# Chunked attention, a gated MLP and a routed expert layer in one program: the first block's vector work in a fixed order

## Chip, cores and metric

The program runs on one core of a Trainium2 chip. The metric is device time in microseconds (us): the median of three runs of the whole program.

## The reference, cut to what matters

```python
# attention inside chunks of 64 tokens: q, k, v are [8, 8, 576, 64]
attn = softmax(q_c @ k_c.T / sqrt(64)) @ v_c          # 4608 tokens x 512
# a dense gated layer, w_in 512 x 2048, w_out 2048 x 512, both in float64
h = x @ w_in
g = h * (1.0 / (1.0 + np.exp(-1.702 * h)))
x = (g @ w_out).astype(np.float32)
# routed layer: tokens with x @ w_skip > 0 go through one of 8 experts
out[do_compute] = xc + gate_w * (relu(xc @ w1[e]) @ w2[e])
```

The change touches the dense layer's first block of tokens and the conversion of its float64 weights that runs beside it.

## The kernel before, in words

The 4608 tokens are cut into 9 blocks of 512. For every block `j` the dense layer runs 16 rounds `i`, one per 128 columns of `w_in`. A round is `emit_h` (12 matmuls of 512 columns into a PSUM bank, L296, then a tanh on ACT, L299, and a multiply on VectorE, L300, which give `sg`), `emit_g` (ACT rounds `sg` to a high part `gh`, L306; VectorE takes the low part `gl`, L307) and, one round later in the program's text, `emit_y` (8 matmuls with `gh`, L316 and L317, and 4 with `gl`, L320). Each product is made of three because values and weights are split into a high and a low part. There are two PSUM banks for `h`, so `h` of round i+2 can start only when L300 of round i has read its bank.

Attention of the next block goes along in some rounds (1, 4, 7, 10 and 13 of block 0). Around a round k of these stand: `a` in round k-1 (8 transposes on TensorE, L141, two copies on ACT, L143), `burst` in round k (the value products of the group before, L207, and the scores of this one, L158; then maxima and differences on VectorE, L166 and L168, the exponential on ACT, L173, and two copies on ACT, L212), and in round k+2 the normalisation `c0` on VectorE (L176 to L179) and `c1` (4 transposes on TensorE, L187, a copy on ACT, L189). All of these PSUM results share two banks, tag `at`.

In block 0 the 32 weight halves (`class Half`: even ones a slice of `w_in`, odd ones of `w_out`) are turned from float64 into two float32 parts, one step ("tick") each. A half needs a load of 512 KB on SP's queue (three buffers), `s0` (two ACT instructions: `r`, L255, and `lf`, L256), `s1` (VectorE shift, L262, and combine, L263, then an add on POOL, L264) and `s3` (ACT rounds to `whi`, L276; VectorE subtracts to `wlo`, L277). Tick m does `s1` of half m, `s0` of half m+1, `s3` of half m-1 and starts the load of half m+3. Before the change six ticks are named in the prologue, and two in each round of block 0 until the 33 are used up.

The program is built in a framework whose scheduler takes the instructions in the order named and may move them: each engine gets an order that the scheduler makes at build time from its own idea of when things are ready. On the chip every engine then runs its own list strictly from first to last.

Of the kernel before, what the change touches and what calls it, by code (L numbers as in the profile page):

```python
# [9 lines left out]
F32 = mybir.dt.float32  # L10
# [11 lines left out]
def kernel(  # L22
# [14 lines left out]
    PE, ACT, DVE, POOL, SP = nc.tensor, nc.scalar, nc.vector, nc.gpsimd, nc.sync  # L37
# [5 lines left out]
    P = 128  # L43
# [3 lines left out]
    NF = DFF // P  # L47
    BT = 512
    TPB = BT // P
# [11 lines left out]

    BURSTS = {0: (1, 4, 7, 10, 13)}
    BURSTN = (1, 5, 9, 13)
    NXT = NT // SL + NE + NSING + 2
    BIG = float(1 << 20)

# [4 lines left out]
    mp = ctx.enter_context(tc.tile_pool(name="main", bufs=1))  # L71
# [7 lines left out]
    def bank(shape, tag, name):  # L79
# [10 lines left out]
        fill=0.0, base=0, channel_multiplier=-1,  # L90
# [13 lines left out]
    emeta = cp.tile([1, 2, NE], U32, name="emeta")  # L104
    meta = cp.tile([1, 3, NXT], U32, name="meta")
    wgT = cp.tile([P, KD, NE + 1], F32, name="wgT")
# [123 lines left out]
    HW = KD * P  # L230

    class Half:
# [14 lines left out]
        def s0(self):  # L247
            bits = self.raw.bitcast(U32).rearrange("p (n two) -> p n two", two=2)
            self.hw = bits[:, :, 1]
            hwf = self.raw.bitcast(F32).rearrange("p (n two) -> p n two", two=2)[:, :, 1]  # L250
            self.r = mp.tile([P, HW], F32, tag="x2", name="r", bufs=4)
            self.lf = mp.tile([P, HW], F32, tag="junk", name="lf")


            ACT.activation(out=self.r, in_=hwf, func=AF.Abs, scale=2.0 ** -112)  # L255
            ACT.activation(out=self.lf.bitcast(U32), in_=bits[:, :, 0], func=AF.Copy, scale=2.0 ** -29)  # L256

        def s1(self):
# [3 lines left out]
            DVE.tensor_scalar(ru, ru, 3, None, op0=ALU.logical_shift_left)  # L262
            DVE.scalar_tensor_tensor(au, self.hw, 0x80000000, ru, op0=ALU.bitwise_and, op1=ALU.bitwise_or)  # L263
            POOL.tensor_tensor(au, au, self.lf.bitcast(U32), op=ALU.add)  # L264

        def s2(self):
            pass

        def s3(self):
            i, h = self.i, self.half  # L270
# [29 lines left out]
        DVE.scalar_tensor_tensor(sg, sg, 1.0, ps, op0=ALU.add, op1=ALU.mult)  # L300
        return sg

    def emit_g(sg):
        gh = mp.tile([P, BT], F32R, tag="gh", name="gh", bufs=2)
        gl = mp.tile([P, BT], F32R, tag="gl", name="gl", bufs=2)
        ACT.activation(out=gh, in_=sg, func=AF.Copy, scale=0.5)  # L306
        DVE.scalar_tensor_tensor(gl, sg, 0.5, gh.bitcast(F32), op0=ALU.mult, op1=ALU.subtract)  # L307
        return gh, gl

# [127 lines left out]
    def extras():  # L437
# [4 lines left out]
        def m2s(shape, nm, dt=F32):  # L442
            return m2.tile(shape, dt, name="x_" + nm)

        def wide(nm):
            t = m2.tile([P, DM], F32, tag="o", name=nm, bufs=2)
            return t[0:1, 0:NXT * NB2].rearrange("o (x b) -> o x b", b=NB2)

        xb = [1, NXT, NB2]
        rem, tu = m2s([1, NE], "rem"), m2s([1, NE], "tu", U32)  # L450
        bc, b0, b1 = m2s([1, 1, NB2], "bc"), m2s([1, 1, NB2], "b0"), m2s([1, 1, NB2], "b1")
        row0, dp = m2s([1, 1, NB2], "row0"), m2s([1, 1], "dp")
        ix, bj, cx = m2s([1, NXT, 1], "ix"), m2s([1, NXT, 1], "bj"), m2s([1, NXT, 1], "cx")

# [77 lines left out]
    def load_next():  # L532
        if cnt["load"] < len(wq):
            s, n, w = wq[cnt["load"]]
            cnt["load"] += 1
            single = s >= NFIRST + NPAIR and w == 0
            raw2.append((s, n, w, None if single else load_w2(expert(s), n, w)))
# [107 lines left out]
    fp = fstack.enter_context(tc.tile_pool(name="f64", bufs=1))  # L645

    def new_x1():
        return [mp.tile([P, 2, BT], F32, tag="x1", name="x1", bufs=2) for _ in range(2)]
# [24 lines left out]
    halves = [Half(m) for m in range(2 * NF)]  # L673
# [18 lines left out]
    tick_n = [0]  # L692

    def tick():
        m = tick_n[0]
        tick_n[0] += 1
        if m == 0:
            halves[0].s0()
        if m < 2 * NF:
            halves[m].s1()  # L700
        if 1 <= m <= 2 * NF:
            halves[m - 1].s2()
        if m + 1 < 2 * NF:
            halves[m + 1].s0()
        if 1 <= m <= 2 * NF:
            halves[m - 1].s3()
        if m + 3 < 2 * NF:
            halves[m + 3].load()

    for tau in range(TPB + 3):  # L710
        if 0 <= tau - 2 < TPB:
            A[tau - 2].c0()
        if tau < TPB:
            A[tau].a()
        if 0 <= tau - 1 < TPB:
            A[tau - 1].b()
        if 0 <= tau - 2 < TPB:
            A[tau - 2].c1()
        if 0 <= tau - 3 < TPB:
            A[tau - 3].d()  # L720
        if tau >= 1:
            tick()
    for g in range(2):
        SP.dma_start(out=tv[g], in_=z)
# [2 lines left out]
    fill, late = [], []  # L727
# [3 lines left out]
    for j in range(NB - 1):  # L731
        for i in BURSTS.get(j, BURSTN):
            round_of[j * NF + i] = len(round_of)
# [4 lines left out]
    for j in range(NB):  # L738
        lastb = j + 1 == NB
        if not lastb:  # L740
            x1 = new_x1()
        else:
            rs.close()
            rawp = rs.enter_context(tc.tile_pool(name="raw", bufs=2, side="right", reuse_waits="tile"))
            for _ in range(4):
                load_next()
        ys = [bank([P, DM], "y", "yps") for _ in range(TPB)]
        prev = None
        nf = len(fill)
        for i in range(NF):  # L750
            R = j * NF + i
            nc_ = round_of.get(R - 2)
            if nc_ is not None and nc_ < NST:
                St[nc_].c0()
            sg = emit_h(i, xh, xl)
            span = NF // 2 - 2 if lastb else NF - 5
            nfill = -(-len(fill) // (span - i)) if i < span else 0
            if nfill:
                fill.pop(0)()
                nfill -= 1  # L760
            if j == 0:
                tick()
                if i == 7:
                    gate_load()
                elif i == 11:
                    gate_rows()
            g = emit_g(sg)
            if prev is not None:
                emit_y(i - 1, prev, ys)
            na = round_of.get(R + 1)  # L770
            if na is not None and na < NST:
                St[na].a()
                if na + 1 < NST:
                    St[na + 1].load_qk()
            if nc_ is not None and nc_ < NST:
                St[nc_].c1()
            kb = round_of.get(R)
            if kb is not None:
                if kb:
                    St[kb - 1].x1 = x1  # L780
                burst(St[kb] if kb < NST else None, St[kb - 1] if kb else None)
                if kb < NST:
                    St[kb].load_v()
            if j == 0:
                tick()
            for _ in range(nfill):
                fill.pop(0)()
            if late and (i >= span or late[0][0] < j):
                late.pop(0)[1]()
            if lastb:  # L790
                if prev is not None:
                    conv_next2()
                if i == NF // 2:
                    gstack.close()
                    m2 = ctx.enter_context(tc.tile_pool(name="m2", bufs=1, reuse_waits="tile"))
                    for s in range(NEARLY):
                        slots[s].list(first_row(s))
                if i >= NF // 2 + 2 and i - NF // 2 - 2 < NEARLY:
                    slots[i - NF // 2 - 2].gather((NB - 1) * BT)
            prev = g  # L800
        if j == 0:
            while tick_n[0] <= 2 * NF:
                tick()
            fstack.close()
            gstack = ExitStack()
            gp = gstack.enter_context(tc.tile_pool(name="gates", bufs=1, reuse_waits="tile"))
            wg = gp.tile([P, NE, DM], F32, name="wg")
            ws = gp.tile([P, DM], F32, name="ws")
            SP.dma_start(out=ws, in_=w_skip.rearrange("(o d) -> o d", o=1).to_broadcast([P, DM]))
            SP.dma_start(  # L810
                out=wg, in_=wgd[0:NE].rearrange("(o e) d -> o e d", o=1).to_broadcast([P, NE, DM]))
        if not lastb:
            xhn = split_x1(x1)
            emit_y(NF - 1, prev, ys)
            xh, xl = xhn
        else:
            slots[0].trans()
            emit_y(NF - 1, prev, ys)
            conv_next2()
        xs = evac_y(j, ys)  # L820
        lg = new_lg()
        if not lastb:
            fill = [lambda t=t, e=e, lg=lg, xs=xs: dot(lg, xs, t, e) for t in range(TPB) for e in range(NE + 1)]
            rt = route(j, lg)
            if j == NB - 3:
                rt.insert(3, order)
            late += [(j + 1, f) for f in rt]


    jx = m2.tile([1, NXT, 1], F32, name="jx")  # L830
    jw = m2.tile([1, NXT, 1], F32, name="jw")
    jm = m2.tile([1, NXT, 1], F32, name="jm")
# [103 lines left out]
```

## Time and profile before

| what | value |
|---|---|
| time, three runs | 1224.11, 1224.36, 1226.07 us; median 1224.36 |
| profiled execution | 1227.84 us, of which the span is 1226.1 us |
| TensorE busy, share of the span | 1182.7 us, 96% |
| VectorE, ACT, POOL | 783.9, 490.2, 144.6 us |

The profiled execution is 3.48 us above the median of the runs. TensorE is near full from about 60 us to the end; the slices that are not full lie in the first 160 us, the prologue and block 0. Block 0's first `h` matmul stands at 48.73 us.

### The profile page before, as it was taken

Reading aid. Unit: us, or ns where it says so; the run is one execution under the profiler, and the core shown is the slowest. Engines: PE = TensorE matmul, PEld = TensorE weight load, DVE = VectorE, ACT = ScalarE, POOL = GpSimd, SP = SyncE. Lnnn points to the kernel's source line nnn. Section 1 sums busy time; section 2 is a strip of 40 time slices with the busy share of each in tenths; the row PEclk is TensorE's granted clock in tenths of the full one; section 3 lists DMA queues with packets and bytes.
Section 4 is the critical chain, followed back from the end, with each engine's and each line's share of the span. In section 5 each row is a group of like instructions: output and inputs, shape, how many; then the busy total and the mean of one; then the engine's idle time right before and its main releaser. Section 6 shows DMA issues by size and latency. Waiting matters only on the chain. (4 is left out here: it accounts for less than half of the span.)

```text
span 1226.1 us, 20893 instructions
## 1 busy us (share of the span) xinstructions
PE 1182.7 (96%) x7984; PEld 991.8 (81%) x7984; DVE 783.9 (64%) x1771; ACT 490.2 (40%) x825; POOL 144.6 (12%) x137
## 2 busy tenths in 40 slices
PE   6798999999999999999999999999999999999995
PEld 4576788888888888888888888888788989999885
DVE  5889578369349548647736935943985686665531
ACT  5867443343332333324334333332344454444320
POOL 2344000010010010000001001001021023231110
PEclk9999999999999999999999999999999999999998
DMA  9756331131122113113113113202344677666540
GB/s 211 208 175 178 112 102 27 44 104 26 27 68 78 28 31 107 32 31 95 35 36 104 26 28 92 55 10 69 130 139 131 215 170 265 215 228 227 195 144 8
DMA packets 181848, 129.00 MB, mean 105 GB/s; under 512 B 122336, under 2 KB 155360, under 8 KB 181617
## 3 DMA queue, kind: packets, MB, share of 16 engines
q1 hardware_dynamic: 177072, 117.09, 33.4%
q0 software_dynamic: 4672, 10.54, 2.5%
q8 instruction: 64, 1.05, 0.4%
q14 instruction: 40, 0.32, 0.1%
HBM read 103.59 MB, written 25.04 MB: 105 GB/s over the span
## 5 line engine op out<-in xcount | busy, mean ns | idle before, releaser
L316 PE MATMUL yps<-whi,gh 128*128 128x512 f32 x576 | 228.7, 397 | 6.4 <-ACT gh L306 6.4
L296 PE MATMUL hps<-xh,whi 128*128 128x512 f32 x576 | 231.6, 405 | 3.2 <-DVE sg L300 3.2
L296 PE MATMUL hps<-xl,whi 128*128 128x512 f32 x576 | 227.5, 395 | 0.0
L296 PE MATMUL hps<-xh,wlo 128*128 128x512 f32 x576 | 227.0, 394 | 0.0
L317 PE MATMUL yps<-wlo,gh 128*128 128x512 f32 x576 | 225.6, 392 | 0.0
L300 DVE SCALAR_TENSOR_TENSOR sg<-sg,hps 128x512 f32<-128x512 f32 x144 | 98.3, 684 | 172.1 <-ACT sg L299 171.1
L353 DVE CUSTOM_DVE_ANT_0 junk<-x,wg 128x512 f32<-128x512 f32 x256 | 175.8, 687 | 4.0
L543 DVE TENSOR_TENSOR elo<-rawe,ehi 128x1024 fp32r<-128x1024 f32 x88 | 107.6, 1224 | 84.6 <-ACT ehi L542 84.5
L320 PE MATMUL yps<-whi,gl 128*128 128x512 f32 x576 | 156.0, 393 | 0.0
L299 ACT ACTIVATE sg<-hps 128x512 f32<-128x512 f32 x144 | 85.8, 598 | 163.4 <-PE hps L296 163.2
L542 ACT CAST ehi<-rawe 128x1024 fp32r<-128x1024 f32 x88 | 92.3, 1049 | 139.6 <-PE h2p L608 69.4
L306 ACT ACTIVATE gh<-sg 128x512 fp32r<-128x512 f32 x144 | 91.0, 632 | 118.3 <-DVE sg L300 104.8
L316 PEld LDWEIGHTS yps<-whi,gh 128*128 128x128 f32 x576 | 108.3, 188 | 30.9 <-ACT gh L306 7.8
L296 PEld LDWEIGHTS hps<-xh,whi 128*128 128x128 f32 x576 | 108.5, 190 | 26.3 <-DVE sg L300 4.1
L296 PEld LDWEIGHTS hps<-xh,wlo 128*128 128x128 f32 x576 | 108.9, 189 | 22.6
L320 PEld LDWEIGHTS yps<-whi,gl 128*128 128x128 f32 x576 | 108.0, 189 | 22.6 <-DVE gl L307 0.3
L317 PEld LDWEIGHTS yps<-wlo,gh 128*128 128x128 f32 x576 | 108.5, 188 | 21.8
L296 PEld LDWEIGHTS hps<-xl,whi 128*128 128x128 f32 x576 | 109.2, 190 | 20.6
L307 DVE SCALAR_TENSOR_TENSOR gl<-sg,gh 128x512 fp32r<-128x512 f32 x144 | 99.0, 688 | 33.4 <-ACT gh L306 21.7
L406 POOL DMA_INDIRECT tab<-pr,pos x36 | 37.8, 1049 | 682.3 <-DVE st L166 335.0
L608 PE MATMUL h2p<-xT,ehi 128*128 128x256 f32 x640 | 117.2, 283 | 0.0
L608 PEld LDWEIGHTS h2p<-xT,ehi 128*128 128x128 f32 x640 | 101.9, 191 | 2.6
(172 smaller groups left out, 1520.5 us busy)
## 6 DMA issues: line engine op xcount, KB each, us to landing
rawe<-in_moe_w_dram SPq DMA_DIRECT2D x88, 512.0 KB, 4.0
v<-in_v_dram SPq DMA_DIRECT2D x144, 64.0 KB, 2.7
x2d<-x SPq DMA_DIRECT2D x36, 256.0 KB, 3.1
out_dram<-x SPq DMA_DIRECT2D x36, 256.0 KB, 3.8
q<-in_q_dram SPq DMA_DIRECT2D x32, 256.0 KB, 3.7
k<-in_k_dram SPq DMA_DIRECT2D x32, 256.0 KB, 3.7
raw<-in_moe_w_in_dram SPq DMA_DIRECT2D x16, 512.0 KB, 4.0
raw<-in_moe_w_out_dram SPq DMA_DIRECT2D x16, 512.0 KB, 3.3
```

The costliest lines, as they stand in the source:

```text
L296: PE.matmul(ps, a, b[:, kk], start=(n == 0), stop=(n == 3 * KD - 1))
L299: ACT.activation(out=sg, in_=ps, func=AF.Tanh, scale=0.851)
L300: DVE.scalar_tensor_tensor(sg, sg, 1.0, ps, op0=ALU.add, op1=ALU.mult)
L306: ACT.activation(out=gh, in_=sg, func=AF.Copy, scale=0.5)
L307: DVE.scalar_tensor_tensor(gl, sg, 0.5, gh.bitcast(F32), op0=ALU.mult, op1=ALU.subtract)
L316: PE.matmul(ys[t], gh[:, cs], wh, start=first, stop=False)
L317: PE.matmul(ys[t], gh[:, cs], wl, start=False, stop=False)
L320: PE.matmul(ys[t], gl[:, cs], wh, start=False, stop=last)
L353: DVE.tensor_tensor_reduce(junk, xs[t], wg[:, e, :] if e < NE else ws, 1.0, 0.0, ALU.mult, ALU.add, lg[:, t, e:e + 1])
L542: ACT.copy(out=hi, in_=raw)
L543: DVE.tensor_tensor(lo, raw, hi.bitcast(F32), op=ALU.subtract)
L608: PE.matmul(ps[:, f], a[:, c], self.xT[:, b, kk], start=(m == 0), stop=(m == 3 * KD - 1))
```

## The change

From the start of block 0 to its end ACT, VectorE and POOL keep their instructions in the order in which the program names them; TensorE and SP are still ordered by the scheduler. Eight ticks instead of six are named in the prologue; the other 25 are dealt evenly over rounds 0 to 14 of the 16 (two, two, one, two, two, one and so on). A round's first tick is named in two parts, `tick1` (`s1`) between `gh` and `gl` and `tick2` (`s3`, `s0`, load) after `gl`; a second tick follows the attention's copies and stands before `burst`. Odd halves get another buffer for `lf`.

```diff
+    NTICK0 = 8
...
-            self.lf = mp.tile([P, HW], F32, tag="junk", name="lf")
+            pool, tag = ((mp, "junk"), (fp, "lf"))[self.half]
+            self.lf = pool.tile([P, HW], F32, tag=tag, name="lf")
...
-    def emit_g(sg):
+    def emit_g(sg, between=None):
...
         ACT.activation(out=gh, in_=sg, func=AF.Copy, scale=0.5)
+        if between is not None:
+            between()
         DVE.scalar_tensor_tensor(gl, sg, 0.5, gh.bitcast(F32), op0=ALU.mult, op1=ALU.subtract)
...
+    def tick1():
         m = tick_n[0]
-        tick_n[0] += 1
         if m == 0:
             halves[0].s0()
         if m < 2 * NF:
             halves[m].s1()
+
+    def tick2():
+        m = tick_n[0]
+        tick_n[0] += 1
         if 1 <= m <= 2 * NF:
-            halves[m - 1].s2()
+            halves[m - 1].s3()
         if m + 1 < 2 * NF:
             halves[m + 1].s0()
-        if 1 <= m <= 2 * NF:
-            halves[m - 1].s3()
         if m + 3 < 2 * NF:
             halves[m + 3].load()
+
+    def ticks_by(i):
+
+        return min(2 * NF + 1, NTICK0 - (-(2 * NF + 1 - NTICK0) * (i + 1) // (NF - 1)))
...
         if tau >= 1:
+            tick()
+        if tau > TPB:
             tick()
...
+        inorder = ExitStack()
+        if j == 0:
+            assert tick_n[0] == NTICK0
+            inorder.enter_context(tc.manual_schedule(engines={ACT.engine, DVE.engine, POOL.engine}))
         for i in range(NF):
...
+            mid = None
             if j == 0:
-                tick()
...
+                if tick_n[0] < ticks_by(i):
+                    mid = tick1
+            g = emit_g(sg, mid)
+            if mid is not None:
+                tick2()
...
             if nc_ is not None and nc_ < NST:
                 St[nc_].c1()
+            while j == 0 and tick_n[0] < ticks_by(i):
+                tick()
...
-            if j == 0:
-                tick()
```

What this does to the engines' lists is seen at three places. In the changed kernel's lists some lines have other numbers: L258 and L259 are `r` and `lf`, L265 and L266 shift and combine, L309 is `gl`, L145, L191, L214 the attention's copies on ACT, L168 and L170 its maxima and differences, L318, L319 and L322 `y`, L189 the transposes of `c1`, L209 the value products.

ACT, the stretch that holds the copy of `c1`'s transposes. Before, around the second of these copies in block 0 (L189):

```order
L143 COPY kT<-kTp 128x512
L255 ACTIVATE r<-raw_1190 128x512
L306 ACTIVATE gh<-sg 128x512
L256 ACTIVATE lf<-raw_1162 128x512
L276 CAST whi<-a 128x512
L256 ACTIVATE lf<-raw_1190 128x512
L276 CAST whi<-a 128x512
L255 ACTIVATE r<-raw_1220 128x512
L299 ACTIVATE sg<-hps 128x512
L189 COPY qT<-pTp 128x512
L256 ACTIVATE lf<-raw_1220 128x512
L255 ACTIVATE r<-raw_1252 128x512
```

In the changed kernel, round 3 from its first tick on, and the head of round 4:

```order
L276 CAST whi<-a 128x512
L258 ACTIVATE r<-raw_662 128x512
L259 ACTIVATE lf<-raw_662 128x512
L145 COPY qT<-qTp 128x512
L145 COPY kT<-kTp 128x512
L191 COPY qT<-pTp 128x512
L276 CAST whi<-a 128x512
L258 ACTIVATE r<-raw_723 128x512
L259 ACTIVATE lf<-raw_723 128x512
L299 ACTIVATE sg<-hps 128x512
L306 ACTIVATE gh<-sg 128x512
```

Before, a tanh (L299) stood ahead of the copy; now the three attention copies stand together, and the tanh of round 4 stands behind them and behind a whole tick.

TensorE, the transposes of `c1` that this copy waits for. Before, the same group's transposes (L187) stand inside an `h`; after that `h` come a whole `y`, the rest of the next `h`, and only then the value products:

```order
L296 MATMUL hps<-xl,whi 128x512
L296 MATMUL hps<-xh,wlo 128x512
L187 MATMUL pTp<-ident,qT 128x128 x4
L296 MATMUL hps<-xh,whi 128x512
L296 MATMUL hps<-xl,whi 128x512
L296 MATMUL hps<-xh,wlo 128x512
L316 MATMUL yps<-whi,gh 128x512
```

In the changed kernel, between `h` of round 5 and `y` of round 3 ahead, and `h` of round 6 behind:

```order
L318 MATMUL yps<-whi,gh 128x512
L319 MATMUL yps<-wlo,gh 128x512
L322 MATMUL yps<-whi,gl 128x512 x4
L189 MATMUL pTp<-ident,qT 128x128 x4
L209 MATMUL sv_881<-qT,v 64x64
```

The transposes moved behind `h` of round 5 and `y` of round 3, and the value products now follow them at once.

VectorE, a round with two ticks and a burst. Before, around the second burst:

```order
L300 SCALAR_TENSOR_TENSOR sg<-sg,hps 128x512
L263 SCALAR_TENSOR_TENSOR a<-raw_940,r 128x512
L262 TENSOR_SCALAR r<-r 128x512
L277 TENSOR_TENSOR wlo<-a,whi 128x512
L307 SCALAR_TENSOR_TENSOR gl<-sg,gh 128x512
L263 SCALAR_TENSOR_TENSOR a<-raw_970,r 128x512
L262 TENSOR_SCALAR r<-r 128x512
L166 TENSOR_REDUCE st<-sv_853 128x4
L166 TENSOR_REDUCE st<-sv_854 128x4
L277 TENSOR_TENSOR wlo<-a,whi 128x512
L168 TENSOR_TENSOR qT<-sv_853,st 128x2x2x64
L168 TENSOR_TENSOR qT<-sv_854,st 128x2x2x64
```

In the changed kernel, round 4:

```order
L300 SCALAR_TENSOR_TENSOR sg<-sg,hps 128x512
L265 TENSOR_SCALAR r<-r 128x512
L266 SCALAR_TENSOR_TENSOR a<-raw_723,r 128x512
L309 SCALAR_TENSOR_TENSOR gl<-sg,gh 128x512
L277 TENSOR_TENSOR wlo<-a,whi 128x512
L265 TENSOR_SCALAR r<-r 128x512
L266 SCALAR_TENSOR_TENSOR a<-raw_773,r 128x512
L277 TENSOR_TENSOR wlo<-a,whi 128x512
L168 TENSOR_REDUCE st<-sv_881 128x4
L168 TENSOR_REDUCE st<-sv_882 128x4
L170 TENSOR_TENSOR qT<-sv_881,st 128x2x2x64
L170 TENSOR_TENSOR qT<-sv_882,st 128x2x2x64
```

Both ticks now stand ahead of the burst's four instructions, and each combine follows the shift of its own half.

## Rows read from the trace of the kernel before

**Rows 1.** Busy time by stretch: start:end, length, each engine's busy us, clock, DMA.

```profile
57.50:119.00 61.50, 54.54 (x345) 42.50 (x346) 56.80 (x87) 44.73 (x81) 30.94 (x20) 0.97 0.61 180
119.00:146.60 27.60, 26.87 (x189) 21.59 (x190) 17.39 (x29) 15.07 (x29) 3.08 (x3) 1.00 0.23 54
```

**Rows 2.** Timeline of TensorE: start, length, engine, line, operation, [idle before <- releaser].

```profile
78.88 0.50 PE L316 MATMUL yps<-whi,gh 128*128 128x512 f32 x1 [2.99 <-ACT gh L306]
...
79.92 0.63 PE L316 MATMUL yps<-whi,gh 128*128 128x512 f32 x1
```

**Rows 3.** Timeline of block 0's end and of its first L300.

```profile
57.54 1.27 DVE L300 SCALAR_TENSOR_TENSOR sg<-sg,hps 128x512 f32<-128x512 f32 x2
...
165.54 1.07 PE L320 MATMUL yps<-whi,gl 128*128 128x512 f32 x4
```

**Rows 4.** Timeline of the prologue's end, ACT, TensorE and VectorE.

```profile
41.67 0.67 ACT L255 ACTIVATE r<-raw 128x512 f32<-128x512 f32 x1 [1.04 <-DMA raw<-in_moe_w_out_dram]
...
43.73 1.12 PE L207 MATMUL pv<-bA,v 64*64 64x64 f32 x16 [2.58 <-ACT x L212]
...
47.25 1.15 ACT L285 CAST xh<-x 128x512 fp32r<-128x512 f32 x2
48.34 2.38 DVE L286 TENSOR_TENSOR xl<-x,xh 128x512 fp32r<-128x512 f32 x2
```

**Rows 5.** Timeline of ACT and VectorE: a tanh, the multiply and the rounding.

```profile
124.48 0.61 ACT L299 ACTIVATE sg<-hps 128x512 f32<-128x512 f32 x1
125.13 0.69 DVE L300 SCALAR_TENSOR_TENSOR sg<-sg,hps 128x512 f32<-128x512 f32 x1 [0.77 <-ACT sg L299]
125.85 0.63 ACT L306 ACTIVATE gh<-sg 128x512 fp32r<-128x512 f32 x1 [0.75 <-DVE sg L300]
```

**Rows 6.** Timeline of TensorE: an `h` and a `y` on end, and `c1`'s transposes.

```profile
67.17 0.39 PE L296 MATMUL hps<-xh,whi 128*128 128x512 f32 x1
...
72.61 0.39 PE L296 MATMUL hps<-xh,whi 128*128 128x512 f32 x1
...
99.93 0.60 PE L187 MATMUL pTp<-ident,qT 128*128 128x128 f32 x4
```

**Rows 7.** Timeline of ACT: instructions that follow each other without a wait.

```profile
35.75 0.67 ACT L255 ACTIVATE r<-raw 128x512 f32<-128x512 f32 x1 [0.55 <-DMA raw<-in_moe_w_out_dram]
36.33 0.67 ACT L256 ACTIVATE lf<-raw 128x512 uint32<-128x512 uint32 x1
36.91 0.35 ACT L212 COPY x<-pv 128x256 f32<-128x256 f32 x1
37.16 0.58 ACT L143 COPY kT<-kTp 128x512 f32<-128x512 f32 x1
```

**Rows 8.** Timeline of VectorE and POOL: two ticks, and the adds beside them.

```profile
79.16 0.68 DVE L263 SCALAR_TENSOR_TENSOR a<-raw,r 128x512 uint32<-128x512 uint32 x1
79.76 0.68 DVE L307 SCALAR_TENSOR_TENSOR gl<-sg,gh 128x512 fp32r<-128x512 f32 x1
...
79.98 1.60 POOL L264 TENSOR_TENSOR a<-a,lf 128x512 uint32<-128x512 uint32 x1 [1.63 <-ACT whi L276]
...
80.36 1.77 DVE L277 TENSOR_TENSOR wlo<-a,whi 128x512 fp32r<-128x512 f32 x1
82.06 0.41 DVE L262 TENSOR_SCALAR r<-r 128x512 uint32<-128x512 uint32 x1
82.39 0.68 DVE L263 SCALAR_TENSOR_TENSOR a<-raw,r 128x512 uint32<-128x512 uint32 x1
83.00 0.68 DVE L277 TENSOR_TENSOR wlo<-a,whi 128x512 fp32r<-128x512 f32 x1
```

**Rows 9.** Timeline of VectorE: attention's maxima and differences, and a normalisation.

```profile
117.96 0.74 DVE L168 TENSOR_TENSOR qT<-sv,st 128x256 f32<-128x256 f32 x2
...
119.93 0.67 DVE L176 TENSOR_REDUCE st<-qT 128x8 f32<-128x512 f32 x1
...
121.69 0.69 DVE L277 TENSOR_TENSOR wlo<-a,whi 128x512 fp32r<-128x512 f32 x1
```

More of the change, by code (lines that the diff above doesn't have):

```diff
@@ L264, in s1 @@
             POOL.tensor_tensor(au, au, self.lf.bitcast(U32), op=ALU.add)
-        def s2(self):
-            pass
         def s3(self):
@@ L694, in tick @@
     def tick():
+        tick1()
+        tick2()
+    def tick1():
         m = tick_n[0]
-        tick_n[0] += 1
         if m == 0:
@@ L748 @@
         prev = None
-        nf = len(fill)
+        inorder = ExitStack()
+        if j == 0:
+            assert tick_n[0] == NTICK0
+            inorder.enter_context(tc.manual_schedule(engines={ACT.engine, DVE.engine, POOL.engine}))
         for i in range(NF):
@@ L766 @@
                     gate_rows()
-            g = emit_g(sg)
+                if tick_n[0] < ticks_by(i):
+                    mid = tick1
+            g = emit_g(sg, mid)
+            if mid is not None:
+                tick2()
             if prev is not None:
@@ L800 @@
             prev = g
+        inorder.close()
         if j == 0:
-            while tick_n[0] <= 2 * NF:
-                tick()
+            assert tick_n[0] == 2 * NF + 1
             fstack.close()
```

## Prediction

> **What bounds the kernel now.** I read the busy times by stretch first. From 57.5 to 119 us TensorE is busy 54.54 of 61.5 us, VectorE 56.80, and the granted clock is 0.97; from 119 to 146.6 us TensorE is busy 26.87 of 27.6 us and VectorE only 17.39 [rows 1]. So TensorE is the bound of the program, but in block 0 it loses 6.96 + 0.73 = 7.7 us to waits, nearly all while the weights are being converted. The largest wait is 2.99 us for `gh`; soon after it a matmul takes 0.63 us [rows 2], where one of the same shape elsewhere takes 0.39 [rows 6]. That is the lower of the clock's two levels, 1.2 GHz, and 0.03 of 61.5 us, about 1.8 us, is what it costs. About 9.5 us is therefore all that a better order can win inside block 0. The first L300 stands at 57.54 us and block 0's last `y` ends at 165.54 + 1.07 = 166.61 us [rows 3]; these dates I compare with those of the changed kernel.
>
> **The prologue.** ACT rounds the first block's input at 47.25 us and VectorE has the first low part at about 48.34 + 0.68 = 49.0 us [rows 4]. Ahead of it ACT waits for the load of half 7, until 41.67 us [rows 4]. SP's list is the same up to there, so this wait stays. After it the new order of ACT has lf, a copy, whi, two copies and then the rounding, without two more halves and a wait for POOL. In row lengths: lf at 42.25, copy 42.83, whi 43.08, copy 43.59; the last copy needs value products that wait for the bank which the copy of 42.83 frees at 43.2, 1.12 us of them [rows 4], so it starts at 44.35 and the rounding near 44.7 us. On VectorE half 7's combine ends near 43.5, the add behind it near 45.0, a wlo held by this add 0.55 us later, and the first low part at about 46.2 us, 2.8 us sooner than now. VectorE's next 5 us also lose a conversion and the fifth group's four score instructions, which I price at 1.2 us. I put the first L300 at 53.5 us: **4.0 us gained**, with 2 and 5 as ends.
>
> **The rounds.** From here three lists are fixed, and I follow one L300 to the next, because `h` of round i+2 waits for L300 of round i. Handoffs come from one stretch: a tanh of 0.61 us ends at 125.09 and L300 starts 0.04 later; L300 lasts 0.69, and ACT goes on 0.03 after it [rows 5]. An `h` and a `y` on end take 72.61 - 67.17 = 5.44 us, `c1`'s transposes 0.60 [rows 6]. ACT issues its next instruction some 0.1 us before the last ends: 0.58 us after r and after lf, 0.25 after a copy of 0.35 [rows 7]. Full copy, whi and exponential, of 0.58, 0.61 and 0.63 us, I take alike: 0.48, 0.51, 0.53.
>
> *Chain A, round 3 to 4 (and 6 to 7).* By the order, TensorE has h5, y3, `c1`'s transposes on end; h5 needs L300 of round 3. ACT has the copy of these transposes, whi, r, lf, and only then round 4's tanh. L300 0.69, handoff 0.04, h5 and y3 5.44, transposes 0.60, handoff 0.04, copy 0.48, whi 0.51, r 0.58, lf 0.58, tanh 0.61, handoff 0.04: **9.61 us** from L300 to L300. Behind the waiting copy on ACT is that whole tick, on VectorE the wlo that needs its whi, on TensorE h6, which needs the next L300.
>
> *Chain B, round 4 to 5.* VectorE: L300 (0.60 to the next), shift 0.41 and handoff 0.04, so the combine starts at 1.05. The pattern combine, gl, wlo is in the trace: wlo ends 80.36 + 1.77 - 79.16 = 2.97 us after the combine's start, because it stands until POOL's add ends, and the next instruction starts 2.90 after it [rows 8]. A wlo straight behind its combine takes 0.68 us, 0.61 after it [rows 8]. So: second shift at 3.95, combine 4.40, wlo 5.01, maxima 5.61, differences 6.27 to 7.01 (0.74 a pair [rows 9], 0.66 apart). Then ACT: exponential 7.05, two copies, tanh 8.08 to 8.69, L300 at **8.73 us**.
>
> *Chain C, round 5 to 6.* One tick: to 3.95 as above, then the normalisation, 121.69 - 119.93 = 1.76 us [rows 9]: **5.71 us**.
>
> Three rounds take 9.61 + 8.73 + 5.71 = 24.0 us, 8.0 a round. TensorE's own work in them is 3 x 5.44 plus three sets of transposes (1.8) and the small products (about 1.2, estimated from rows 4), 19.3 us. It would stand still for some 4.7 us in each three rounds.
>
> **The sum.** Round 0 has the two tick parts and two copies of transposes: by the same steps 6.2 us to the next L300; round 1 is chain B without block copies, 8.2; round 2 is chain C, 5.7. L300 of round 3 at 53.5 + 20.1 = 73.6 us; of round 9 at 121.6. Round 9 to 10 is chain A with `y` of round 9 itself ahead of the transposes, 0.7 longer, so round 12 at 146.3. Round 12 to 13 has one `y` in place of `h` and `y`: 7.5; 13 to 14 chain B: 162.5. Then gh (1.4 after L300), y14, a next-block h, 8 transposes, another h, y15 with 3 more matmuls and 2 transposes inside: 1.4 + 4 x 2.72 + 1.2 + 0.7 + 0.3 = 14.5, and block 0's last `y` ends at 177.0 us. That is 10.4 later than 166.61. By then 9 matmuls (2.05 us at 5.44/24) and 2 transposes (0.3) more of the next block are done, so the loss is **8.0 us**. What follows waits for TensorE and moves along. The profiled execution, 1227.84, would become 1235.8; it lies 3.48 over the median of 1224.36, so I forecast **1232.4 us**. No change that I can tell from none is 0.2%, 2.4 us.
>
> Costed at nothing: the second `lf` buffer, and the loads. A load starts when its buffer's combine is done and ACT wants it two ticks later, 6 us or more by the chains; in between SP may wait for a group's transposes or value products. If that cover goes, ACT's r is late by what the load is late, as at 41.67 us, where it waited 1.04 us [rows 4].
>
> **The rivals.**
>
> *Faster: TensorE's pace.* If `y` stays two rounds behind `h`, TensorE has 10 us of work in hand, and ACT and VectorE, with about 14 us of issue each in three rounds by the lengths above, could keep up. Then the 7.7 us of waits and 1.8 of clock go, the start brings 4.0, and 1.2 of group transposes comes into the block: 1224.4 - 12.3 = 1212 us. Against it: chain A is closed by the lists whatever the durations, since h5 and y3 stand ahead of the transposes. It decides only if chain A is under 7 us. Chance 0.12.
>
> *Level: the adds don't hold VectorE.* If wlo behind gl took its 0.68 us, chains B and C lose 1.1 us each; over fourteen rounds about 10 us, and the result is near 1222 to 1223. Rows 8 speak against it, and this pattern now stands in fourteen rounds, so I give it 0.19: 0.12 inside 0.2%, 0.06 faster, the rest slower. The Trainium skill, "SBUF — State Buffer", section "Who interferes with whom", has VectorE and GpSimd share a port pair that the first to issue keeps for its whole instruction; by that rule the wlo is held whatever its place. The trace agrees: the held wlo ends 0.55 us after the add [rows 8].
>
> *Slower still: the clock.* Chain A leaves TensorE with small products and waits for some 4 us, and the next group's transposes wait for two PSUM banks until the burst's copies. A wait like it dropped the clock [rows 2]. After the burst the loss would lie in a wait that is there anyway; behind the group's transposes it would lengthen the way to h8 by about 1.4 us in three or four places: 1237 us, 0.10. If every gap dropped it and nothing hid that, nine gaps at 1.8 us add 16 us: 1248 us; but with 6.96 us of waits the clock lost only 0.03 in 61.5 us [rows 1], so 0.02. [...]
>
> **How the numbers follow.** The forecast has 0.57 (1227 to 1238: chain lengths are good to 0.3 us each, the start to 1.5), the clock 0.12, the adds 0.19, TensorE's pace 0.12. Slower: 0.57 + 0.12 + 0.01 = 0.70. Within 0.2%: 0.12. Faster: 0.12 + 0.06 = 0.18. The range, 1219 to 1242 us, leaves out most of TensorE's pace and the worst of the clock.
>
> **What would show it.** Right: in the stretch 70 to 150 us TensorE waits before the value products for the copy of `c1`'s transposes, before h6 for L300, before the group's transposes for the burst's block copies; ACT waits two to three us for TensorE ahead of that copy; L300s are 9.6, 8.7, 5.7 us apart; TensorE busy about 80%; the first L300 near 53.5 us. Wrong: TensorE over 90% busy there, or wlo behind gl at 0.7 us, or equal steps of 6.4 us between L300s.

## Result and the profile after

The changed kernel takes 1239.99 us (median of four runs, 1237.60 to 1240.44) against 1225.21 us for the kernel before in the same comparison: **1.14% slower**, ratio 1.0114 with a 95% interval of 1.0101 to 1.0126; the medians are 14.8 us apart. The forecast of 1232.4 us has the right sign, the time lies inside the range, and the loss is 1.8 times what was forecast.

The profiled execution took 1239.68 us with a span of 1237.8 us. Its busy times by stretch (start:end, length, busy us of PE, PEld, DVE, ACT and POOL, granted clock, DMA share, GB/s), which answer to [rows 1]:

```profile
75.00:99.00 24.00, 19.74 (x148) 15.50 (x147) 17.99 (x30) 14.10 (x27) 7.62 (x5) 1.00 0.52 143
99.00:123.00 24.00, 19.72 (x142) 15.67 (x141) 18.06 (x29) 14.16 (x28) 7.59 (x5) 0.93 0.50 143
123.00:147.00 24.00, 20.82 (x150) 16.75 (x149) 16.72 (x27) 14.70 (x28) 7.84 (x5) 0.93 0.45 128
```

No engine is full. TensorE, busy 89% from 57.5 to 119 us before, is at 82% in the first two of these stretches, VectorE at 75% where it had 92%, and nobody else took over: the time lies in waits between the engines. This is what a closed chain looks like in such a table.

The chain itself is seen in the dates of L300 (timeline of VectorE, rounds 0 to 6; the two left out, of rounds 1 and 2, stand at 59.33 and 67.63 us, and there are no others in the stretch):

```profile
53.20 0.69 DVE L300 SCALAR_TENSOR_TENSOR sg<-sg,hps 128x512 f32<-128x512 f32 x1 [4.91 <-ACT sg L299]
...
73.38 0.68 DVE L300 SCALAR_TENSOR_TENSOR sg<-sg,hps 128x512 f32<-128x512 f32 x1
83.13 0.69 DVE L300 SCALAR_TENSOR_TENSOR sg<-sg,hps 128x512 f32<-128x512 f32 x1 [0.94 <-ACT sg L299]
91.97 0.69 DVE L300 SCALAR_TENSOR_TENSOR sg<-sg,hps 128x512 f32<-128x512 f32 x1 [1.79 <-ACT sg L299]
97.71 0.68 DVE L300 SCALAR_TENSOR_TENSOR sg<-sg,hps 128x512 f32<-128x512 f32 x1
```

The steps are 9.75, 8.84 and 5.74 us, and they come again: 9.70, 8.84, 5.72 in the next three rounds. One such period in TensorE's timeline, with all its waits:

```profile
81.00 0.73 PE L209 MATMUL sv<-qT,v 64*64 64x64 f32 x29 [0.68 <-ACT qT L191]
...
83.88 0.50 PE L296 MATMUL hps<-xh,whi 128*128 128x512 f32 x1 [1.61 <-DVE sg L300]
...
91.22 0.66 PE L143 MATMUL qTp<-ident,q 128*128 128x128 f32 x4 [1.57 <-ACT x L214]
...
92.71 0.50 PE L296 MATMUL hps<-xh,whi 128*128 128x512 f32 x1 [0.40 <-DVE sg L300]
```

0.68 + 1.61 + 1.57 + 0.40 = 4.26 us in 24.3. The first two belong to chain A. On ACT (timeline) the copy of `c1`'s transposes stands 2.98 us for TensorE, then come `whi`, `r` and `lf`, and only then the tanh, while TensorE, once its value products are done, can only wait for its L300:

```profile
80.36 0.58 ACT L191 COPY qT<-pTp 128x512 f32<-128x512 f32 x1 [2.98 <-PE pTp L189]
80.84 0.62 ACT L276 CAST whi<-a 128x512 fp32r<-128x512 f32 x1
81.36 0.70 ACT L258 ACTIVATE r<-raw 128x512 f32<-128x512 f32 x1
81.96 0.65 ACT L259 ACTIVATE lf<-raw 128x512 uint32<-128x512 uint32 x1
82.51 0.59 ACT L299 ACTIVATE sg<-hps 128x512 f32<-128x512 f32 x1
```

The other two belong to chain B. Its VectorE list (timeline of VectorE and POOL) has the `wlo` behind `gl` held to 1.79 us beside POOL's add, where [rows 8] had 1.77:

```profile
84.80 0.68 DVE L309 SCALAR_TENSOR_TENSOR gl<-sg,gh 128x512 fp32r<-128x512 f32 x1
85.06 1.59 POOL L267 TENSOR_TENSOR a<-a,lf 128x512 uint32<-128x512 uint32 x1 [5.11 <-ACT whi L276]
85.41 1.79 DVE L277 TENSOR_TENSOR wlo<-a,whi 128x512 fp32r<-128x512 f32 x1
```

Where the time went is read from one mark that is the same in both kernels, the first copy of a block's `y` on ACT. In the kernel before, blocks 0 and 1 have it at

```profile
165.97 1.08 ACT L326 COPY x<-yps 128x512 f32<-128x512 f32 x2 [5.50 <-PE yps L320]
265.31 1.08 ACT L326 COPY x<-yps 128x512 f32<-128x512 f32 x2 [1.93 <-PE yps L320]
```

and in the changed kernel at

```profile
177.84 1.07 ACT L328 COPY x<-yps 128x512 f32<-128x512 f32 x2 [0.50 <-PE yps L322]
276.10 1.08 ACT L328 COPY x<-yps 128x512 f32<-128x512 f32 x2 [1.93 <-PE yps L322]
```

It is late by 11.87 us at the end of block 0 and by 10.79 at the end of block 1, and by 10.78 still at the end of block 3 (364.36 + 99.05 = 463.41 against 474.19 us). So most of the loss is made in block 0. The spans of these two profiles differ by 11.7 us. Behind that figure stand two things: from the first `y` copy of block 8 to the end the changed kernel takes 2.5 us more (281.66 against 279.14), and 1.6 us had come back on the way there, because the clock fell between blocks 7 and 8 in this profile of the kernel before and not in the changed kernel's.

### The profile page after: what moved, and what is told of

Its sections match the earlier page's. It is cut to its first block, busy times and chain, and to the rows that moved or that the text cites. A ratio compares the mean times of both kernels' runs of the same rounds, so it can differ in the third digit from the quotient of the medians.

```text
span 1237.8 us, 20861 instructions
## 1 busy us (share of the span) xinstructions
PE 1185.6 (96%) x7984; PEld 993.1 (80%) x7984; DVE 787.3 (64%) x1771; ACT 488.5 (39%) x825; POOL 146.6 (12%) x137
## 5 line engine op out<-in xcount | busy, mean ns | idle before, releaser
L318 PE MATMUL yps<-whi,gh 128*128 128x512 f32 x576 | 228.9, 397 | 4.2 <-ACT gh L306 4.2
L319 PE MATMUL yps<-wlo,gh 128*128 128x512 f32 x576 | 225.7, 392 | 0.0
L300 DVE SCALAR_TENSOR_TENSOR sg<-sg,hps 128x512 f32<-128x512 f32 x144 | 98.5, 684 | 181.6 <-ACT sg L299 180.6
L322 PE MATMUL yps<-whi,gl 128*128 128x512 f32 x576 | 155.4, 391 | 0.0
L299 ACT ACTIVATE sg<-hps 128x512 f32<-128x512 f32 x144 | 85.8, 597 | 165.5 <-PE hps L296 165.3
L318 PEld LDWEIGHTS yps<-whi,gh 128*128 128x128 f32 x576 | 108.7, 189 | 28.3 <-ACT gh L306 5.1
L319 PEld LDWEIGHTS yps<-wlo,gh 128*128 128x128 f32 x576 | 108.8, 189 | 22.0
L322 PEld LDWEIGHTS yps<-whi,gl 128*128 128x128 f32 x576 | 107.6, 188 | 22.3
L309 DVE SCALAR_TENSOR_TENSOR gl<-sg,gh 128x512 fp32r<-128x512 f32 x144 | 99.1, 688 | 30.4 <-ACT gh L306 20.3
```

The lines of the kernel that those rows point to most:

```text
L299: ACT.activation(out=sg, in_=ps, func=AF.Tanh, scale=0.851)
L318: PE.matmul(ys[t], gh[:, cs], wh, start=first, stop=False)
L319: PE.matmul(ys[t], gh[:, cs], wl, start=False, stop=False)
L322: PE.matmul(ys[t], gl[:, cs], wh, start=False, stop=last)
```

## The experiments

Two theories stood against each other. **The chains** (the prediction's): the fixed lists of ACT and VectorE close chains A, B and C with TensorE's list. **The work**: 25 conversion ticks spread over 15 rounds, each with a `wlo` held behind an add, are too much for VectorE and POOL in whatever order. First the order alone, in four kernels.

**No fixed order.**

```diff
-            inorder.enter_context(tc.manual_schedule(engines={ACT.engine, DVE.engine, POOL.engine}))
+            pass
```

> The changed kernel with its ticks dealt and split as they are, but without the fixed order: the scheduler orders all engines. Theory (the loss is in the chains that the fixed lists of ACT and VectorE close with TensorE's list): the waits of block 0 go back to about the 7.7 us of the kernel before and the longer prologue brings up to 4 us, so 1219 to 1229 us. Rival (the conversion work itself, 25 ticks spread over 15 rounds with a wlo held behind each POOL add, is too much for VectorE in whatever order): still 1234 us or more.

Measured 1227.59 us (ratio 1.0018, 1.0009 to 1.0028). The ticks are dealt and split as in the changed kernel, and 12.4 of its 14.8 us are gone: the loss is the fixed order's. But the first L300 stands at 58.99 us, so the longer prologue brings no earlier start by itself.

**ACT free, VectorE and POOL fixed.**

```diff
-engines={ACT.engine, DVE.engine, POOL.engine}
+engines={DVE.engine, POOL.engine}
```

> The changed kernel with VectorE and POOL in the order named and ACT left to the scheduler. Theory: ACT's list puts the tanh of the next round ahead of the copy of c1's transposes, so chain A (9.7 us) opens and falls to VectorE's own 5.6 us or TensorE's pace, and chain B (8.8 us) falls to about 7.0, where VectorE's list ends; three rounds then take TensorE's 19.3 us rather than 24.3, and the time is 1222 to 1229 us. Rival (VectorE's list with the held wlo is the cost): it is unchanged, so 1236 to 1241 us.

Measured 1230.04 us (1.0044, 1.0027 to 1.0061), 1 us over what the chains gave and 6 under the rival. Rounds 3 to 12 take 66.46 us against 74.19. The steps are the theory's in the first period alone, 5.63, 7.47 and 6.55 us, 19.7 together; the next two take 23.2 and 23.6 us, with waits of TensorE of 2.94 and 1.74 us for ACT's copies of the attention (L214) that the theory had not named, and the lower clock behind each (0.93 from 99 to 123 and from 123 to 147 us). The start is late too: TensorE's first `h` waits 3.83 us for `xh`, which ACT's free list has late, and the first L300 is at 56.32 us.

**ACT alone fixed.**

```diff
-engines={ACT.engine, DVE.engine, POOL.engine}
+engines={ACT.engine}
```

> The changed kernel with ACT alone in the order named, VectorE and POOL left to the scheduler. Theory: chain A stays at 9.7 us, because it has ACT and TensorE alone in it; chain B falls from 8.8 to about 6 us, since the built list has the burst's maxima and differences straight behind L300; three rounds take about 22 us rather than 24.3, and the time is 1229 to 1235 us. Rival (VectorE's list is the cost): most of the loss goes, 1222 to 1227 us, with L300s about 6.5 us apart.

Measured 1227.72 us (1.0024, 1.0014 to 1.0034). The time is the rival's, within 1 us, but there is no trace of its equal steps of 6.5 us. The periods are the theory's, 21.6, 23.1 and 22.0 us for three rounds where it had about 22; the steps in them are so in part, A at 10.5 to 12.1 us (9.7 expected), B at 6.9 (about 6 expected) and C at 4.2. The rest of the gain, some 3 us, lies behind round 12, where I had expected none: from that L300 to the first `y` copy it takes 27.25 us against 30.27. How B became short is seen on VectorE (timeline of the round with the second burst):

```profile
82.16 0.68 DVE L300 SCALAR_TENSOR_TENSOR sg<-sg,hps 128x512 f32<-128x512 f32 x1
82.76 0.75 DVE L168 TENSOR_REDUCE st<-sv 128x4 f32<-128x256 f32 x2
83.42 0.75 DVE L170 TENSOR_TENSOR qT<-sv,st 128x256 f32<-128x256 f32 x2
84.08 0.68 DVE L309 SCALAR_TENSOR_TENSOR gl<-sg,gh 128x512 fp32r<-128x512 f32 x1
84.68 0.69 DVE L277 TENSOR_TENSOR wlo<-a,whi 128x512 fp32r<-128x512 f32 x1
```

Maxima and differences stand straight behind L300; shift and combine were done ahead of it, POOL's add (82.41 to 83.68 us) runs beside L300 and the maxima, which take no longer for it, and the `wlo` meets no add. So neither list alone makes the loss: with either of them free, 10 to 12 us come back.

**The second tick ahead of the copies**, all three engines fixed: one term of chain A alone.

```diff
+            while j == 0 and tick_n[0] < ticks_by(i):
+                tick()
             na = round_of.get(R + 1)
...
                 St[nc_].c1()
-            while j == 0 and tick_n[0] < ticks_by(i):
-                tick()
```

> The changed kernel with a round's second tick named ahead of the attention's copies, not behind them, so that no whi, r and lf stand between the copy of c1's transposes and the next tanh; all three engines stay in the order named. Theory: chain A loses whi, r and lf, 1.67 us, and takes about 8.0 us in four places, so about 5 to 7 us less, 1233 to 1236 us. Rival (amount of conversion work on VectorE): the work and VectorE's list are the same, 1238 to 1241 us.

Measured 1238.50 us (1.0112, 1.0095 to 1.0129): by the time a miss, and inside the rival's range. By the steps chain A falls from 9.75 and 9.70 to 8.07 us, by whi, r and lf as worked out, with B and C as they were (8.87, 5.75):

```profile
80.56 0.58 ACT L191 COPY qT<-pTp 128x512 f32<-128x512 f32 x1 [0.69 <-PE pTp L189]
81.04 0.60 ACT L299 ACTIVATE sg<-hps 128x512 f32<-128x512 f32 x1
```

L300 of round 12 comes 5.28 us sooner than in the changed kernel. Then 2.2 us go back in one step: from round 12 to 13 it takes 9.91 us, not 7.68, because TensorE's list, built anew, has the next `h` ahead of the transposes there, and this `h` waits for a conversion:

```profile
148.06 0.50 PE L296 MATMUL hps<-xh,wlo 128*128 128x512 f32 x1 [0.83 <-DVE wlo L277]
```

At the end of block 1 the gain is 3.06 us, in the profiled executions 2.9 (1236.75 against 1239.68), in the medians 1.5.

Next the other term, a version with both, and each of the two kernels again.

**The adds left out**, all three engines fixed.

```diff
-            POOL.tensor_tensor(au, au, self.lf.bitcast(U32), op=ALU.add)
```

> The changed kernel, all three engines in the order named, with the 32 POOL adds left out (the weights lack the part that lf carries; everything else is done). It prices the hold of wlo behind the add. Theory: a wlo behind gl takes 0.6 us of VectorE's list instead of 1.7, so chain B falls from 8.8 to about 7.7 and chain C from 5.7 to about 4.6; B and C together are then TensorE's own 13.3 us rather than 14.6, chain A stays at 9.7, and the time is 1231 to 1236 us. Rival (the hold is all that the fixed order of VectorE costs): the time comes to that with VectorE left to the scheduler, 1226 to 1229 us. Rival (VectorE's list does not set the pace): 1238 us or more.

Measured 1231.94 us (1.0055, 1.0033 to 1.0077), as the chains had it. B is 7.74 us and C 4.65, each 1.1 less; A grows to 10.5, because TensorE is now behind by what B and C no longer leave it, and the period is 22.9 us where 9.7 + 13.3 = 23.0 was expected. Without the add ACT's `whi` also has no add to wait for; that this is not what counts is seen on the `wlo` itself, which is 1.10 us shorter, as much as B and C are. The same two instructions as above (here L308 and L276):

```profile
82.69 0.69 DVE L308 SCALAR_TENSOR_TENSOR gl<-sg,gh 128x512 fp32r<-128x512 f32 x1
83.29 0.69 DVE L276 TENSOR_TENSOR wlo<-a,whi 128x512 fp32r<-128x512 f32 x1
```

**ACT alone fixed, and the second tick ahead of the copies** (the edits of two kernels above together).

> ACT alone in the order named, and a round's second tick ahead of the attention's copies. Theory: what is left of the loss with ACT alone fixed is chain A, which again loses whi, r and lf, 1.67 us, in three places; 1222 to 1225 us, at or under the kernel before. Rival (TensorE's list, which the scheduler builds anew, takes it back, as it did at the fourth place with all three fixed): 1226 to 1229 us.

Measured 1225.62 us against 1226.08 (0.9997, 0.9987 to 1.0007): level with the kernel before, so by the time between the two. Steps of 8.8, 7.5 and 4.7 us, 21.0 a period; its block 0 is the shortest of all, with block 1's first `y` copy at 261.20 us, 4.1 and 2.8 ahead of the two profiles of the kernel before. This lead is gone at the end, though neither theory has a loss there. From block 8's `y` copy to the end it takes 281.19 us, against 279.14 and 279.46 in the two profiles of the kernel before: TensorE waits 2.9 us for gathered tokens where it was 1.6, and just behind that wait, at 1189 us, the clock falls, which it does at that place in neither profile of the kernel before. It also falls between blocks 7 and 8, as in the first of those two profiles and not in the second. Why the wait is longer stays open.

**Both kernels profiled again.** No edit.

> The kernel before, profiled a second time. Its first profiled execution lay 2.3 us over the median of its runs. Theory: that excess lies in the prologue or the tail, where DMA decides, and block 0's waits of 7.7 us and its clock of 0.97 to 0.98 come again; rival: it lies in block 0 (another clock, other waits), so that the loss of the change in block 0, 10.8 us by the first pair of profiles, has to be read with that much uncertainty.

The execution took 1225.27 us, 2.57 less than the first. Block 0 is the same: 108.43 and now 108.53 us from the first L300 to the `y` copy, so the rival falls. 1.4 us are there at the first L300 (56.16 against 57.54 us), in the prologue as expected; another 1.6 lies where I had named nothing, between the `y` copies of blocks 7 and 8 (87.73 against 89.33 us). The granted clock settles that part: from 857 to 867 us it is 0.83 in the first execution and 1.00 in this one (rows in the last section).

> The changed kernel, profiled a second time. Theory (the lists close the chains): the steps between L300s repeat to 0.1 us, 9.7, 8.8 and 5.7 us, but for steps in which the clock falls; the clock falls behind waits, at the same two places (117 and 134 us), about 1.7 us each. Rival: the falls of the clock come elsewhere or not at all, and block 0 ends 1.5 to 3.5 us sooner or later.

The execution took 1239.44 us. The steps repeat to 0.04 us where the clock stays, 9.73, 8.84, 5.74, then 9.73, 8.82, 5.75. The clock fell elsewhere, as the rival had it, and once, not twice; but block 1's `y` copy is only 0.6 us later than in the first profile, not 1.5 to 3.5 (stretch and TensorE's timeline of this profile):

```profile
99.00:123.00 24.00, 21.32 (x148) 16.70 (x147) 18.01 (x29) 14.46 (x27) 7.59 (x5) 0.93 0.51 143
123.00:147.00 24.00, 18.94 (x147) 14.68 (x146) 17.41 (x27) 14.91 (x28) 7.87 (x5) 1.00 0.44 125
```

```profile
109.32 0.50 PE L296 MATMUL hps<-xh,whi 128*128 128x512 f32 x1 [1.61 <-DVE sg L300]
...
110.04 0.63 PE L296 MATMUL hps<-xh,wlo 128*128 128x512 f32 x1
```

Four pairs of executions put block 1's `y` copy later by 10.8, 11.4, 12.1 and 12.7 us, mean 11.7.

**The start alone.** Can the early start be had without the loss? Three kernels fix ACT's order only in the first rounds.

```diff
-engines={ACT.engine, DVE.engine, POOL.engine}
+engines={ACT.engine}
...
             prev = g
-        inorder.close()
+            if i == 0:
+                inorder.close()
```

> The changed kernel with the order fixed for ACT alone and in round 0 alone; from round 1 on the scheduler orders every engine. Theory (the gain at the start and the loss in the rounds come apart: the first comes of ACT's order up to the rounding of the first input and the first tanh, the second of fixed lists in rounds 3 to 14): the first L300 at 53 to 54 us, from there to block 0's first y copy about the 108.5 us of the kernel before, so 1221.5 to 1223.5 us, faster than both kernels. Rival (the scheduler builds the rest anew and gives the gain back in other waits): 1224.5 to 1228 us.

Measured 1231.59 us (1.0044, 1.0027 to 1.0061). With `i == 1` in place of `i == 0`:

> The same with ACT's order fixed in rounds 0 and 1. Theory: as with round 0 alone, 1221.5 to 1224 us. Rival: 1224.5 to 1228 us.

Measured 1230.38 us (1.0038, 1.0024 to 1.0052). And the kernel before with eight ticks in the prologue and the same two pieces of code around round 0:

> The kernel before, with its own dealing of two ticks to each round and its undivided tick, eight ticks in the prologue, and ACT's order fixed in round 0 alone; neither the even dealing nor the split tick nor the second lf buffer. Theory (the start's gain needs only ACT's order): the first L300 at 53 to 54.5 us and 1221.5 to 1224 us. Rival (it needs the even dealing, because two undivided ticks in round 0 hold VectorE): the first L300 at 56 us or later, 1225 us or more.

Measured 1226.21 us (1.0011, 1.0001 to 1.0021). By the time my theory fell in all three; the first two lie over their rivals' ranges as well, and the third has the early L300 of the theory with the time of its rival. The first L300s are early, at 54.00, 54.23 and 51.93 us, and nothing of that is left at the end. One stretch behind the start, of the kernel with round 0 alone fixed:

```profile
75.00:99.00 24.00, 19.28 (x133) 13.73 (x132) 23.83 (x35) 17.18 (x32) 10.75 (x8) 0.93 0.71 203
```

VectorE is full, 23.83 of 24 us, and TensorE stands still for 4.7 of them, 3.32 at one place, for a `gh` whose L300 came late. I read it so that the scheduler puts the conversions as early as they can go, and a TensorE that starts sooner only meets a full VectorE sooner. No run tests this, and a full VectorE alone does not tell the kernels apart: the kernel before has 23.56 of 24 us there in its second profile, with TensorE busy 20.92.

**Both terms away at once**, all three engines fixed: no adds, and the tick ahead of the copies.

> All three engines in the order named, the POOL adds left out (the weights lack the part that lf carries) and a round's second tick ahead of the attention's copies: both terms at once. Theory (the fixed lists cost nothing but these two terms, the tick behind the copy in chain A and the held wlo in chains B and C): A about 8.6 to 8.9, B 7.7, C 4.6, 21.0 us in three rounds, which is TensorE's own work and two short waits, as with ACT alone fixed and the tick ahead of the copies; 3 x 3.4 us less than the changed kernel over rounds 3 to 12 and some 2 less in rounds 0 to 3, so 1227 to 1230 us. Rival (the two terms don't add, one covers the other): no better than with the adds alone left out, 1231 to 1233 us.

Measured 1227.40 us against 1226.58 (1.0007, 0.9998 to 1.0017). Steps of 8.9, 7.75 and 4.65 us, 21.3 a period. With all three lists fixed by hand and these two things out of them, the loss is gone to within the measurement. The readings together:

| kernel | A, B, C, us | rounds 3 to 12, us | block 1's first y copy | time, us |
|---|---|---|---|---|
| before, two profiles | no fixed pattern | 60.5, 60.5 | 265.31, 264.04 | 1225.2 |
| changed, two profiles | 9.7, 8.8, 5.7 | 74.2, 73.6 | 276.10, 276.70 | 1240.0 |
| tick ahead of copies | 8.1, 8.9, 5.7 | 68.7 | 273.04 | 1238.5 |
| adds left out | 10.5, 7.7, 4.6 | 70.8 | 269.81 | 1231.9 |
| both | 8.9, 7.75, 4.65 | 63.9 | 263.81 | 1227.4 |
| ACT alone fixed | 10.5 to 12.1, 6.9, 4.2 | 66.8 | 265.02 | 1227.7 |
| the same, tick ahead | 8.8, 7.5, 4.7 | 63.0 | 261.20 | 1225.6 |

## Why the prediction was right, and its size wrong

**The bound: right.** TensorE's share in block 0 decides, and the loss is its waits.

**The prologue: right as a date.** First L300 at 53.20 us, 53.5 forecast. The gain of 4.0 us was taken against one execution; with both profiles of each kernel (57.54 and 56.16, 53.20 and 54.35) it is 3.1 us. It was the wrong mark, though: the row in [rows 3] says x2 and 1.27 us, so two L300s stand back to back there, round 1's at about 58.1 us, and the changed kernel has that one at 59.33. In the kernel before TensorE had done two `h` by then and waited for VectorE. By round 1 nothing is gained, which fits the kernels with only the start fixed.

**The chains: right, to 0.15 us.** A 9.61 forecast, 9.75 and 9.70 measured; B 8.73 and 8.84; C 5.71 and 5.74. 4.7 us of waits in three rounds were forecast and 4.26 measured. Two runs take single terms out of them and move each step by what the working says: whi, r and lf 1.67 us in A, the held `wlo` 1.1 us in B and C.

**The sum: too small by 7.6 us**, 1239.99 against 1232.4. It divides so:

- *"it lies 3.48 over the median ..., so I forecast 1232.4"*: this step failed, by 3.5 us. I took the distance of one profiled execution from the median for a property of the kernel. It belonged to that execution: a second one of the same kernel took 1225.27 us, with 1.4 us less in the prologue and 1.6 less between blocks 7 and 8, where the clock had fallen in the first; and the changed kernel's two, 1239.68 and 1239.44, lie under its median.
- *"By then 9 matmuls ... and 2 transposes ... more of the next block are done"*, 2.35 us: mis-sized. The lag falls only by 1.1 us from block 0's `y` copy to block 1's, in all four pairs, 1.25 us more loss.
- *Rounds 3 to 12*, 72.7 us forecast, 74.19 and 73.63 measured: 0.9 to 1.5 us more. Some 0.6 us is the chains' steps, each 0.03 to 0.15 longer than forecast; most of the rest is the step from round 9 to 10, 11.04 and 10.44 where 10.3 was forecast, and the 0.6 us between these two I put down to the clock (below). *Rounds 12 to 14*: 16.5 against 16.2. Start and end of block 0 were right, 53.20 against 53.5 and 14.40 against 14.5 us.
- *"What follows waits for TensorE and moves along"*: right to the last stage, which the sum took as unchanged. From block 8's `y` copy on it is 1.4 to 2.5 us longer (281.66 and 280.83 us against 279.14 and 279.46). TensorE's wait for the gathered tokens is 2.8 us there (2.3 in the second profile) where it was 1.6 in both profiles of the kernel before, and behind it the clock falls in both profiles of the changed kernel, 1.7 us each, and in neither of the kernel before (rows in the last section). The two can account for it; why the wait grew was not tried.

**The rivals.** *TensorE's pace* fell: 82% busy, steps of 9.7, not 6.4. *The adds don't hold VectorE* fell: the `wlo` takes 1.79 us, 0.69 without the add, and taking all adds out brings 8 us, where I had put 10. By the rule of the Trainium skill, "SBUF — State Buffer", section "Who interferes with whom", every `wlo` that starts behind the add is held; the runs agree. *The clock* came true in part. The profile of after shows 0.93 in two stretches of 24 us, 1.7 us each, the first behind a group's transposes, as that rival had it:

```profile
115.50 0.66 PE L143 MATMUL qTp<-ident,q 128*128 128x128 f32 x4 [1.60 <-ACT x L214]
...
116.99 0.51 PE L296 MATMUL hps<-xh,whi 128*128 128x512 f32 x1 [0.40 <-DVE sg L300]
...
117.72 0.63 PE L296 MATMUL hps<-xh,wlo 128*128 128x512 f32 x1
```

From 117.72 to 120.28 us matmuls start 0.43 us apart and not 0.23, the lower level, 1.2 GHz; by the second profile some 0.6 us of it reached L300 of round 10. The worst case, every gap, did not come, though the pattern of waits is the same in each period.

## What to carry to other kernels

Before fixing an order by hand, follow one buffer around: which instruction frees it, what stands ahead of that on each engine's list, and add it up; a chain that is closed by the lists gave its period here to 0.3 us in 24 from a trace that never ran it. Keep movable work (here a whole conversion tick) out from behind an instruction that waits for another engine and ahead of the one that this engine waits for, and don't let the instruction behind a POOL operation be one that it holds. And make the sum against the runs' median, or profile twice: the distance of one execution from it is no property of the kernel.

## What the runs showed of the hardware

**What a POOL add holds.** Over the profiles, instructions of VectorE that start behind an add (1.3 to 1.8 us) while it runs on POOL fall into two kinds. Held, so that they end 0.55 us behind the add where they alone take 0.68: `wlo`, `gl`, the combine and the normalisation's product, all with two inputs in SBUF. Held in the same way are the shift, which has one input (0.42 us alone, 1.52 held), and even the addition of a constant to 128x8 (0.17 alone, 0.96 held). Not held: L300 and the differences, with an input in PSUM, and the reductions and the reciprocal. With ACT alone fixed and the tick ahead, VectorE's timeline has this beside an add that ran from 88.32 to 89.60 us:

```profile
88.67 0.96 DVE L179 TENSOR_SCALAR st<-st 128x8 f32<-128x8 f32 x1
```

An instruction of 8 columns waits for one of 512. What stands behind an add on VectorE's list decides the price, not how much work it is.

It is the later of the two that waits. Where VectorE is first, the add is held, and by one instruction after the other. In the first profile of the kernel before (timeline of VectorE and POOL):

```profile
59.34 0.42 DVE L262 TENSOR_SCALAR r<-r 128x512 uint32<-128x512 uint32 x1
59.56 4.09 POOL L264 TENSOR_TENSOR a<-a,lf 128x512 uint32<-128x512 uint32 x1 [0.81 <-ACT lf L256]
59.67 0.68 DVE L307 SCALAR_TENSOR_TENSOR gl<-sg,gh 128x512 fp32r<-128x512 f32 x1
60.27 0.68 DVE L277 TENSOR_TENSOR wlo<-a,whi 128x512 fp32r<-128x512 f32 x1
...
62.08 0.42 DVE L262 TENSOR_SCALAR r<-r 128x512 uint32<-128x512 uint32 x1
```

Six instructions of VectorE go through on end at their own lengths, and the add takes 4.09 us in place of 1.3.

The Trainium skill, "SBUF — State Buffer", section "Who interferes with whom", says which kinds these are: with two SBUF inputs an instruction of VectorE contends with one of GpSimd that reads SBUF, and with at most one there is no contention except in the two-port modes, which `tensor_scalar` can enter and `tensor_reduce` cannot on this chip; the rows agree on every kind seen here.

**In block 0 the clock's falls do not follow the order.** The changed kernel, run twice, fell to the lower level behind a wait of 1.60 us that was followed by transposes and another of 0.40, and behind one of 2.28, in one execution; behind one of 1.61 in the other. Three more waits of 1.57 to 1.61 us in the first profile, and the 2.29 us at the same place in the second, changed nothing. At the start of block 0 matmuls of `h` also start 0.43 us apart, until 48.84 us in the first and 51.67 in the second, though the profiles have the granted clock at 1.00 there; the second's first L300 is 1.15 us later. The kernel before has the plainest case, between blocks 7 and 8: the same wait in front of the same matmul, in its first and in its second profile (TensorE's timeline and the stretch, the first profile's two rows ahead):

```profile
861.03 0.50 PE L296 MATMUL hps<-xh,whi 128*128 128x512 f32 x1 [1.84 <-DVE sg L300]
857.00:867.00 10.00, 8.16 (x29) 6.28 (x28) 7.44 (x18) 3.99 (x7) 0.00 (x0) 0.83 0.65 247
...
859.75 0.50 PE L296 MATMUL hps<-xh,whi 128*128 128x512 f32 x1 [1.84 <-DVE sg L300]
857.00:867.00 10.00, 8.16 (x37) 6.42 (x36) 9.75 (x26) 3.70 (x7) 0.00 (x0) 1.00 0.56 211
```

In the last stage the fall came in both profiles of the changed kernel, behind waits of 2.83 and 2.04 us for gathered tokens, and in neither of the kernel before, with 1.30 and 1.24 us at that place. The stretch behind it, changed kernel and kernel before, first profiles:

```profile
1200.00:1210.00 10.00, 8.31 (x48) 7.74 (x49) 0.89 (x3) 1.09 (x3) 1.67 (x2) 0.83 0.17 63
...
1190.00:1200.00 10.00, 8.70 (x61) 7.76 (x60) 1.27 (x3) 1.56 (x4) 1.46 (x2) 1.00 0.16 59
```

A forecast can price such a fall (1.7 us) but, on these rows, not place it in block 0.
